# Where the chunk score products stand in a tick of a fused attention kernel

## The chip, the cores and the metric

The kernel runs on one core of one Trainium2 chip. The metric is the device time of that core in microseconds (us). A core has five engines that each work through a queue of their own, in order: TensorE (PE) for matrix products and transposes, VectorE (DVE), ScalarE (ACT), GpSimd (POOL), and SyncE (SP), from which this kernel issues its DMAs. PE's results go to PSUM; VectorE and ScalarE read PSUM and write SBUF. PEld is the weight load of a product, which can lie beside another product.

## The reference

Three stages on 8 batches of 576 tokens, with 8 heads of 64 (a width of 512). The first is attention within chunks of 64 tokens, without a mask. The second has four experts, each a causal attention over the 576 tokens of its batch with one head of 64; a token takes its two best experts, weighted by a softmax of their gate logits. The third is a layer norm and a network of 512 to 2048 to 512 with a ReLU and a residual.

```python
scores = scale * np.matmul(q_c, k_c.transpose(0, 1, 2, 4, 3))   # chunks of 64
attn = exp(scores - max); attn = attn / (sum(attn) + 1e-09)
x = np.matmul(attn, v_c)                                         # to [B, S, 512]
...
q, k, v = x @ wq[e], x @ wk[e], x @ wv[e]                        # e = 0..3
scores = np.where(causal, -1e9, scale * q @ k.T); a = softmax(scores)
out += mask[..., None] * w[:, :, kk:kk + 1] * (a @ v @ wo[e])    # the two best e
...
xn = (x - mu) / np.sqrt(var + 1e-06) * g_ln
ch = np.maximum(xn @ w_ch1, 0.0) @ w_ch2
return x + ch
```

## The kernel before

The 4608 tokens are 36 tiles of 128. A prologue (a list of steps written out by hand, to about 57 us) works on the first seven tiles; then `tick(s)` runs for s = 7 to 36, one token tile in and one out each time; the network follows, from about 490 us on. What the change touches is `tick`, in the stage from 57 to 445 us.

The pieces of work are Python generators, and `step(g)` lets a generator write its instructions up to its next `yield`. The order in which `tick` calls `step` is thus the order in which the program is written. A scheduler then orders the instructions of each engine, by and large as written but with moves of its own, and puts the waits between engines in. Each engine takes its instructions strictly in the built order.

The generators, with the tiles and lines that the prediction names:

- **Chunk attention of tile g** (`chunk_tile`, L142 to L187) has four steps. The first only takes the loaded tiles. The second writes the score products s_ps (L151, 32 products of 64x64) and the softmax over the chunk: the maximum nmc (L154) and the subtraction pc (L156) on VectorE, the exponential on ScalarE (L157), the sum and its reciprocal lc on VectorE (L159 to L161), and a multiplication on GpSimd (L162). The third transposes pc to pT_ps (L166), copied by ScalarE (pTc, L168). The fourth writes the output products x_ps (L176, 32 products of 64x64), which are taken from PSUM as a high part xTh (ScalarE, L185) and the rest xTl (VectorE, L186). Every product of the later stage is done as three of such parts.
- **Projections of a group of three tiles** (`proj_group`, L193 to L264): steps of 12 products each. A k or q step (pp, L209) ends in an eviction by ScalarE and VectorE (L212, L213 for q, L222, L223 for k), a v step (pv, L233) in L235, L236. After the last v step comes the gate.
- **Expert attention of half a token tile** (`attn_half`, L268 to L358): the two halves are the two pairs of experts. Its steps are the scores sp (L299), mask and maximum in one operation of VectorE (L312, twice), exponentials on ScalarE (L313, twice), VectorE's small l pieces (L314 to L316) and GpSimd's multiplication (L318); transposes tp (L327) with copies on ScalarE and VectorE (L329, L331); products oa_ps (L342), taken as zh and zl (L345, L346); and, in the second of a tile's halves, y_ps (L353, six products: zl with woh, zh with wol, zh with woh, for each of two pairs).
- **Weight conversion** (`narrow`, L365 to L407) goes beside it: the network's weights arrive as 64-bit numbers and are made into 32-bit ones in pieces by VectorE (L373 to L379, L384, L389), GpSimd (L381, L402) and ScalarE (L393). `bg(s)` writes one piece of it. The pieces on VectorE have to stay in the written order among one another.

PSUM has four single buffers for s_ps, pT_ps, pp, pv, tp, oa_ps and y_ps, and two double ones that sp and x_ps share. A product that needs a buffer waits until the last reader of its former content is done.

One tick has two halves. In each half come, in this order: transposes of an earlier expert half, scores of a new one, the y_ps step of a third, the chunk step of tile s, a projection step, the chunk step of tile s - 1, and the oa_ps step, with `bg(s)` between them. In the first half the chunk steps are the taking of the loaded tiles (tile s) and the transposes pT_ps (tile s - 1). In the second half they are s_ps with its softmax (tile s) and x_ps (tile s - 1). The lines are L438 to L454.

Of the kernel before, what the change touches and what calls it, by code (L numbers as in the profile page):

```python
# [22 lines left out]
def tile_kernel(ctx, tc, dims, qkt, vt, wqt, wkt, wvt, wo, g_ln, w_ch1, w_ch2, out):  # L23
# [77 lines left out]
    def load_tile(g):  # L101
        qk = se.tile([128, 2, HP, 128], F32, name="qk", bufs=3)
        vb = se.tile([128, H, D], F32, name="vb", bufs=4)
        nc.sync.dma_start(qk.rearrange("p i a t -> p (i a t)"), qkt[g])
        nc.sync.dma_start(vb.rearrange("p h d -> p (h d)"), vt[g])
        loaded[g] = (qk, vb)
# [305 lines left out]
    def step(gen):  # L412
        if gen is not None:
            next(gen, None)
# [3 lines left out]
    def bg(s, n=1):  # L418
        for _ in range(n):
            if s < CS:  # L420
                return
            if not cgen:
                if not conv:
                    return
                cgen.append(conv.pop(0)())
            if next(cgen[0], 0) == 0:
                cgen.pop()

    def tick(s, fill=None):
        if s + 2 < NT:  # L430
            load_tile(s + 2)
        if s < NT:
            chunks[s] = chunk_tile(s)
        if s >= GT + 1 and (s - GT - 1) % GT == 0 and (s - GT - 1) // GT < NT // GT:
            projs.append(proj_group((s - GT - 1) // GT))
        if s == MID - 1:
            bg(s, 999)
        for half in range(2):  # L438
            h = 2 * (s - LA) + half
            bg(s)  # L440
            step(attn.get(h - LG))
            if 0 <= h < 2 * NT:
                attn[h] = attn_half(h // 2, h % 2)
                step(attn[h])
            bg(s)
            step(attn.pop(h - LG - 1, None))
            step(chunks.get(s))
            bg(s)
            if projs:
                step(projs[0])  # L450
            bg(s)
            step(chunks.get(s - 1))
            bg(s)
            step(attn.get(h - LG))  # L454
            if projs and (s - GT - 1) % GT == 2 and half == 1:
                step(projs[0])
                projs.pop(0)
            if fill is not None:
                fill(s, half)
        chunks.pop(s - 1, None)  # L460
# [8 lines left out]
    chunks = {}  # L469
# [24 lines left out]
    for s in range(LA, MID):  # L494
        tick(s)
# [110 lines left out]
    def fill(s, half):  # L606
        next(beg, None)

    for s in range(MID, TAIL):
        tick(s, fill)  # L610
# [6 lines left out]
    for s in range(TAIL, NT + LA):  # L617
        tick(s, fill)
# [332 lines left out]
```

## Time and profile before

| | |
|---|---|
| time, median of 3 runs | 1266.5 us (1265.26 to 1267.33) |
| time of the profiled execution | 1263.14 us |
| its span in the profile | 1261.4 us |
| PE busy | 1230.1 us, 98% |
| VectorE busy | 907.1 us, 72% |
| ScalarE busy | 594.7 us, 47% |
| GpSimd busy | 265.4 us, 21% |
| granted clock of PE, mean | 0.993 |

The trace is of one execution. All times in it count from the start of the span. A row of a timeline has the start and the duration of an instruction or of a row of like instructions, its engine and line, the operation, what it writes and reads, and in brackets how long the engine stood idle before it and for whom. Products of PE overlap, so the duration of one can reach into the next; start to start is what one costs in a row. A row of waits says which engine, tile and line waited for which, for how long in total, how often, and how long at most. The granted clock is a share of the full 2.4 GHz; 0.50 is 1.2 GHz.

### The profile page before, as it was taken

How to read it: one execution, taken by the hardware profiler on the slowest of the kernel's cores; microseconds unless marked ns; L12 is line 12 of the kernel's file. 1: busy time of each engine (PE TensorE's matmuls, PEld its weight loads, DVE VectorE, ACT ScalarE, POOL GpSimd, SP SyncE). 2: the span in 40 equal slices, each digit the busy share in tenths (PEclk: the TensorE clock that was granted, in tenths of full speed). 3: DMA queues.
4: the chain of work that ended last, by engine and by line, in shares of the span. 5: the costliest groups of instructions: out<-in, count | busy, mean ns of one | idle time of the engine just before them, and what ended most of it. 6: DMA issues, size and time to landing. Idle time of an engine off the chain costs nothing.

```text
span 1261.4 us, 29453 instructions
## 1 busy us (share of the span) xinstructions
PE 1230.1 (98%) x11874; PEld 1149.3 (91%) x11874; DVE 907.1 (72%) x1957; ACT 594.7 (47%) x1171; POOL 265.4 (21%) x480
## 2 busy tenths in 40 slices
PE   7989999999999999999999999999899999999998
PEld 5878888888788887899999999999799999999998
DVE  5578777787866676996567656755797778767783
ACT  3465655566566567643343334335443433324331
POOL 2245444444542223311121202110000000000000
PEclk8999999999999999999999999999999999999999
DMA  7333434434332013655555565558865455554521
GB/s 258 104 130 116 139 116 139 139 107 148 125 106 69 28 50 126 239 196 178 179 176 170 166 196 172 166 156 257 312 200 174 138 165 159 163 175 140 168 93 42
DMA packets 95848, 191.71 MB, mean 152 GB/s; under 512 B 8544, under 2 KB 42336, under 8 KB 94816
## 3 DMA queue, kind: packets, MB, share of 16 engines
q1 hardware_dynamic: 95712, 189.83, 46.3%
q8 instruction: 93, 1.52, 0.5%
q14 instruction: 43, 0.35, 0.1%
HBM read 118.50 MB, written 71.30 MB: 150 GB/s over the span
## 4 chain that ended last, share of the span: by engine, by line
PE 84%; DVE 7%; ACT 3%; DMA 3%; POOL 1%; issue 1%; SPq 0%; DVEq 0%; POOLq 0%; ACTq 0%
PE bb L850 16%; PE bb L660 15%; PE ad L850 12%; PE ad L660 11%; PE pp L209 7%; PE pv L233 4%; PE oa_ps L342 4%; PE tp L327 4%; PE y_ps L353 4%; PE sp L299 3%; PE s_ps L151 2%; DMA w2u<-w2d 1%; PE x_ps L176 1%; PE pT_ps L166 1%; PE tp L554 1%
## 5 line engine op out<-in xcount | busy, mean ns | idle before, releaser
L660 PE MATMUL bb<-x,w1u 128*128 128x256 f32 x1728 | 217.1, 281 | 2.1 <-ACT v L681 1.6
L660 PEld LDWEIGHTS bb<-x,w1u 128*128 128x128 f32 x1728 | 209.6, 188 | 2.9 <-ACT v L681 1.9
L660 PE MATMUL ad<-x,w1u 128*128 128x256 f32 x1296 | 169.6, 282 | 1.9 <-DVE u L684 1.2
L660 PEld LDWEIGHTS ad<-x,w1u 128*128 128x128 f32 x1296 | 159.5, 188 | 2.6 <-DVE u L684 1.4
L850 PE MATMUL bb<-w2u,hn 128*128 128x256 f32 x928 | 160.3, 281 | 0.8 <-DVE xr L860 0.8
L850 PEld LDWEIGHTS bb<-w2u,hn 128*128 128x128 f32 x928 | 134.2, 189 | 1.2 <-DVE xr L860 1.0
L318 POOL TENSOR_SCALAR P<-P,l 128x128 f32<-128x128 f32 (+8 forms) x144 | 93.7, 662 | 163.2 <-DVE l L316 90.5
L850 PE MATMUL bb<-w2u,hx 128*128 128x256 f32 x640 | 125.6, 283 | 0.5 <-DVE hx L815 0.5
L313 ACT ACTIVATE P<-P,nm 128x128 f32<-128x128 f32 (+8 forms) x144 | 87.7, 611 | 72.0 <-DVE nm L312 71.6
L850 PE MATMUL ad<-w2u,hn 128*128 128x256 f32 x632 | 104.4, 281 | 0.0
L850 PEld LDWEIGHTS bb<-w2u,hx 128*128 128x128 f32 x640 | 101.0, 191 | 0.7 <-DVE hx L815 0.7
L381 POOL TENSOR_TENSOR cvt<-cva,cvt 128x512 f32<-128x512 f32 x32 | 44.3, 1385 | 238.5 <-DVE cvt L379 192.2
L850 PEld LDWEIGHTS ad<-w2u,hn 128*128 128x128 f32 x632 | 89.3, 189 | 0.0
L850 PE MATMUL ad<-w2u,hx 128*128 128x256 f32 x504 | 88.9, 280 | 0.0
L402 POOL TENSOR_TENSOR cw<-cw 128x128 f32<-128x128 f32 x128 | 61.3, 494 | 70.3 <-issue 53.6
L850 PEld LDWEIGHTS ad<-w2u,hx 128*128 128x128 f32 x504 | 74.1, 189 | 0.0
L327 PE MATMUL tp<-ident,P 128*128 128x128 f32 x464 | 66.6, 280 | 2.8 <-POOL P L318 2.7
L312 DVE CUSTOM_DVE_ANT_0 P<-sp,mcaus 128x128 f32<-128x128 f32 (+7 forms) x128 | 62.3, 516 | 7.5 <-PE sp L299 7.2
L342 PE MATMUL oa_ps<-pTa,vg 128*64 128x128 f32 x928 | 67.0, 280 | 0.3 <-ACT pTa L329 0.3
L572 DVE TENSOR_TENSOR x<-xt,x 128x512 fp32r<-128x512 f32 x63 | 49.2, 792 | 20.8 <-ACT x L571 20.8
L327 PEld LDWEIGHTS tp<-ident,P 128*128 128x128 f32 x464 | 50.0, 141 | 14.2 <-issue 8.4
L342 PEld LDWEIGHTS oa_ps<-pTa,vg 128*64 128x64 f32 x928 | 49.4, 136 | 10.7 <-issue 6.0
(236 smaller groups left out, 2643.8 us busy)
## 6 DMA issues: line engine op xcount, KB each, us to landing
qk<-in_qk SPq DMA_DIRECT2D x36, 512.0 KB, 4.1
hn<-hd SPq DMA_DIRECT2D x34, 512.0 KB, 4.4
raw<-in_w_ch SPq DMA_DIRECT2D x32, 512.0 KB, 3.9
hx<-hd SPq DMA_DIRECT2D x29, 512.0 KB, 4.4
vb<-in_v SPq DMA_DIRECT2D x36, 256.0 KB, 3.2
xs<-y SPq DMA_DIRECT2D x36, 256.0 KB, 2.0
xc<-xs SPq DMA_DIRECT2D x18, 512.0 KB, 4.6
hd<-p SPq DMA_DIRECT2D x36, 256.0 KB, 4.0
```

What stands on the lines that cost most here:

```text
L209: nc.tensor.matmul(pp, a[:, f, ws], b_[:, f, :], start=(f == 0 and n == 0), stop=(f == KF - 1 and n == 2))
L233: nc.tensor.matmul(pv, a[:, f, cs], b_[:, f, :], start=(f == 0 and n == 0), stop=(f == KF - 1 and n == 2))
L312: nc.vector.tensor_tensor_reduce(dst, src, mk, -1.0, -3.0 * NEG, OP.add, OP.min, nm[:, e2:e2 + 1])
L313: nc.scalar.activation(pe, pe, AF.Exp, bias=nm[:, e2:e2 + 1], scale=-1.0, accum_out=l[:, e2:e2 + 1])
L318: nc.gpsimd.tensor_scalar(P[e2][:, pad:W], P[e2][:, pad:W], l[:, e2:e2 + 1], 1.0, OP.mult, OP.mult)
L327: nc.tensor.transpose(tp[:, i, :], P[e2][:, kt * 128:(kt + 1) * 128], ident)
L342: nc.tensor.matmul(o_ps[e2 * HD:(e2 + 1) * HD, :], vg[:, gk % GT, e * HD:(e + 1) * HD], pT[:, e2 * n + kt, :], start=(kt == 0), stop=(kt = ...
L353: nc.tensor.matmul(y_ps, a[:, e2, :], b_[:, e2, :], start=(e2 == 0 and i == 0), stop=(e2 == EP - 1 and i == 2))
L402: nc.gpsimd.tensor_tensor(w[:, o, :], w[:, x, :], w[:, y, :], op)
L572: nc.vector.tensor_tensor(t[:, 1], tsum[i], f32(t[:, 0]), OP.subtract)
L660: nc.tensor.matmul(out[:, p], w[:, kt, a, WI[i], :], x[:, b_, kt, :], start=(start and p == 0 and kt == 0 and q == 0), stop=False, skip_gr ...
L850: ins = nc.tensor.matmul(to[:, t], x[:, c, ts], w2u[i][:, w, half * 4 + c, :], start=start, stop=False, skip_group_check=True)
```

## The change

```diff
@@ -444,11 +444,11 @@
                 step(attn[h])
             bg(s)
             step(attn.pop(h - LG - 1, None))
-            step(chunks.get(s))
             bg(s)
             if projs:
                 step(projs[0])
             bg(s)
+            step(chunks.get(s))
             step(chunks.get(s - 1))
             bg(s)
             step(attn.get(h - LG))
```

The chunk step of tile s is written behind the projection step, directly ahead of the chunk step of tile s - 1, in both halves. In the first half this moves no instruction of an engine, since that step only takes loaded tiles. In the second half it moves s_ps and the chunk softmax. It applies in the 29 ticks from s = 7 to s = 35. Three places of the built order follow.

PE, the second half of the tick that starts its s_ps at 191 us (s = 17), before:

```order
L299 MATMUL sp<-kWh,qh 128x256 x2
L151 MATMUL s_ps<-qk 64x64 x16
L209 MATMUL pp<-xTl,wqh 128x384
L209 MATMUL pp<-xTh,wql 128x384
L209 MATMUL pp<-xTh,wqh 128x384
...
L176 MATMUL x_ps<-pTc,vb 64x64 x16
L342 MATMUL oa_ps<-pTa,vg 64x128 x2
L327 MATMUL tp<-ident,P 128x128 x4
```

and now:

```order
L299 MATMUL sp<-kWh,qh 128x256 x2
L209 MATMUL pp<-xTl,wqh 128x384
L209 MATMUL pp<-xTh,wql 128x384
L209 MATMUL pp<-xTh,wqh 128x384
...
L151 MATMUL s_ps<-qk 64x64 x16
L176 MATMUL x_ps<-pTc,vb 64x64 x16
L342 MATMUL oa_ps<-pTa,vg 64x128 x2
L327 MATMUL tp<-ident,P 128x128 x4
```

The 12 products of the q step stand ahead of s_ps now, and x_ps stands directly behind it; a row without a number of times stands for one instruction, and the nine q products that are left out repeat the three. Some 20 rows further on, the six products of y_ps stood in one piece ahead of the 12 products of a v step; now eight of these stand between the third and the fourth of y_ps.

VectorE, the second half of the tick at 232 us (s = 20), where conversion pieces (cva, cvt) stand between those of the softmax, before:

```order
L154 TENSOR_REDUCE nmc<-s_ps 128x8
L156 TENSOR_TENSOR pc<-s_ps,nmc 128x512
L314 TENSOR_SCALAR l<-l 128x2
L315 RECIPROCAL l<-l 128x2
L316 TENSOR_TENSOR l<-l,wg 128x2
L373 TENSOR_SCALAR cva<-raw_3553 128x512
L159 TENSOR_REDUCE lc<-pc 128x8
L213 TENSOR_TENSOR ql<-pp,qh 128x384
...
L375 SCALAR_TENSOR_TENSOR cva<-raw_3553,cva 128x512
L186 TENSOR_TENSOR xTl<-x_ps,xTh 128x4x128
L377 TENSOR_SCALAR cvt<-cva 128x512
L346 TENSOR_TENSOR zl<-oa_ps,zh 128x128
```

and now:

```order
L314 TENSOR_SCALAR l<-l 128x2
L315 RECIPROCAL l<-l 128x2
L316 TENSOR_TENSOR l<-l,wg 128x2
L373 TENSOR_SCALAR cva<-raw_3553 128x512
L213 TENSOR_TENSOR ql<-pp,qh 128x384
L375 SCALAR_TENSOR_TENSOR cva<-raw_3553,cva 128x512
L154 TENSOR_REDUCE nmc<-s_ps 128x8
L377 TENSOR_SCALAR cvt<-cva 128x512
L156 TENSOR_TENSOR pc<-s_ps,nmc 128x512
L186 TENSOR_TENSOR xTl<-x_ps,xTh 128x4x128
L379 SCALAR_TENSOR_TENSOR cvt<-raw_3553,cvt 128x512
...
L346 TENSOR_TENSOR zl<-oa_ps,zh 128x128
```

L154 and L156 stood ahead of the three l pieces and stand behind them now, two conversion pieces further on. Between xTl and zl stand L379 and L159 (the row left out) where L377 stood; the two rows left out before are the small lc pieces L160 and L161.

VectorE, the second half of the first tick (s = 7, s_ps at 57 us), before:

```order
L154 TENSOR_REDUCE nmc<-s_ps 128x8
L314 TENSOR_SCALAR l<-l 128x2
L156 TENSOR_TENSOR pc<-s_ps,nmc 128x512
L315 RECIPROCAL l<-l 128x2
L316 TENSOR_TENSOR l<-l,wg 128x2
L213 TENSOR_TENSOR ql<-pp,qh 128x384
L159 TENSOR_REDUCE lc<-pc 128x8
```

and now:

```order
L314 TENSOR_SCALAR l<-l 128x2
L315 RECIPROCAL l<-l 128x2
L316 TENSOR_TENSOR l<-l,wg 128x2
L384 TENSOR_SCALAR cva<-raw_852 128x512
L213 TENSOR_TENSOR ql<-pp,qh 128x384
L389 SCALAR_TENSOR_TENSOR cva<-cva,cvt 128x512
L154 TENSOR_REDUCE nmc<-s_ps 128x8
L312 ISA P,nm<-sp,mcaus 128x256
L312 ISA nm 128x1
L156 TENSOR_TENSOR pc<-s_ps,nmc 128x512
```

L154 stood first in the row and stands behind two conversion pieces and the q eviction now, and L156 behind the first L312 of the half that follows.

No instruction is added or removed. On the queue of SyncE the loads of qk and vb change places with one load of conversion input in seven ticks.

## Rows read from the trace of the kernel before

**Rows 1.** The page, busy time of each engine, share of the span, instructions.

```profile
PE 1230.1 (98%) x11874; PEld 1149.3 (91%) x11874; DVE 907.1 (72%) x1957; ACT 594.7 (47%) x1171; POOL 265.4 (21%) x480
```

**Rows 2.** Waits of PE, 57 to 445 us: total us, times, longest.

```profile
PE sp L299 <- DVE xTl L186: 2.9, 3, 1.0
PE pT_ps L166 <- POOL pc L162: 2.7, 1, 2.7
PE y_ps L353 <- DVE zl L346: 0.7, 3, 0.2
```

**Rows 3.** Chain of waits, 190 to 245 us: start, duration, engine, tile, line.

```profile
192.18 0.69 DVE nmc L154
...
195.88 0.56 DVE cva L375
...
197.87 0.98 PE y_ps L353 x3
...
214.92 1.07 DVE cva L375
```

**Rows 4.** VectorE's groups by line, 57 to 445 us: busy, mean ns, idle before.

```profile
L156 DVE TENSOR_TENSOR pc<-s_ps,nmc 128x512 f32<-128x512 f32 x29 | 20.0, 690 | 0.5
```

**Rows 5.** Table by stretch, L389 alone: length, VectorE busy (times), granted clock, DMA.

```profile
57.00:371.00 314.00, 15.46 (x16) 0.99 0.39 127
```

**Rows 6.** PE's timeline, ticks at 191 and 203 us: start, duration, line, operation.

```profile
190.98 1.15 PE L151 MATMUL s_ps<-qk 64*64 64x64 f32 x32
192.06 0.44 PE L209 MATMUL pp<-xTl,wqh 128*128 128x384 f32 x1
...
194.37 0.69 PE L176 MATMUL x_ps<-pTc,vb 64*64 64x64 f32 x32
195.00 0.44 PE L342 MATMUL oa_ps<-pTa,vg 128*64 128x128 f32 x4
...
200.14 0.60 PE L166 MATMUL pT_ps<-ident,pc 128*128 128x128 f32 x4
```

**Rows 7.** PE's timeline in the prologue.

```profile
23.52 1.08 PE L151 MATMUL s_ps<-qk 64*64 64x64 f32 x29
...
25.07 1.49 PE L97 MATMUL wp<-wz 128*128 128x256 bf16 x12
```

**Rows 8.** Waits of VectorE, 66 to 375 us.

```profile
DVE l L314 <- ACT P L313: 22.0, 22, 1.4
```

**Rows 9.** ScalarE's timeline, ticks at 216 and 232 us.

```profile
219.93 0.19 ACT L313 ACTIVATION_READ_ACCUMULATOR P<-P,nm 128x1 f32 x1
...
234.71 0.19 ACT L313 ACTIVATION_READ_ACCUMULATOR P<-P,nm 128x1 f32 x1
```

**Rows 10.** VectorE's timeline, ticks at 57, 216 and 232 us.

```profile
61.40 0.68 DVE L154 TENSOR_REDUCE nmc<-s_ps 128x8 f32<-128x512 f32 x1
...
223.00 0.69 DVE L186 TENSOR_TENSOR xTl<-x_ps,xTh 128x512 fp32r<-128x512 f32 x1
...
239.37 0.28 DVE L346 TENSOR_TENSOR zl<-oa_ps,zh 128x128 fp32r<-128x128 f32 x1
```

**Rows 11.** PE's timeline, ticks at 57, 69 and 232 us; in brackets a wait.

```profile
66.78 0.66 PE L166 MATMUL pT_ps<-ident,pc 128*128 128x128 f32 x4 [2.66 <-POOL pc L162]
...
73.86 0.69 PE L176 MATMUL x_ps<-pTc,vb 64*64 64x64 f32 x32
...
239.71 0.50 PE L353 MATMUL y_ps<-woh,zl 128*128 128x512 f32 x1
```

**Rows 12.** GpSimd's timeline, tick at 191 us.

```profile
196.03 1.31 POOL L162 TENSOR_TENSOR pc<-pc,lc 128x512 f32<-128x512 f32 x1 [1.03 <-ACT zh L345]
```

**Rows 13.** Table by stretch: PE, PEld, VectorE, ScalarE, GpSimd busy; granted clock; DMA.

```profile
67.00:70.00 3.00, 2.63 (x34) 1.92 (x33) 2.15 (x11) 2.69 (x9) 2.10 (x5) 0.85 0.43 161
70.00:74.00 4.00, 4.00 (x36) 3.64 (x38) 2.67 (x7) 1.09 (x4) 1.50 (x4) 0.68 0.61 206
200.00:250.00 50.00, 48.92 (x607) 41.38 (x605) 38.56 (x118) 30.58 (x79) 24.39 (x42) 1.00 0.42 137
```

## The prediction

> **What bounds the kernel now.** I read the page first: the products of TensorE (PE) are busy for 98% of the span and VectorE (DVE) for 72% [rows 1], so what counts is any time that PE loses or saves. The change touches only the attention stage, about 57 to 445 us. There the list of PE's waits is short, 6.3 us in its three largest lines [rows 2], and these name the places where another engine is only just in time: sp (the scores of the big attention) waits for VectorE's xTl, which frees the PSUM buffer that x_ps filled; pT_ps (the transposes of the chunk softmax) waits for GpSimd's last step; y_ps waits for VectorE's zl. Two of these three are VectorE. The chain of waits of one stretch says the same [rows 3]: it leaves PE after s_ps, goes down VectorE's queue from the chunk softmax (nmc) past the weight conversion (cva), and comes back to PE at y_ps. So the second half of a tick is bound by PE, with VectorE's in-order queue close behind it.
>
> 29 ticks move a chunk (the x29 of L156, [rows 4]). In 20 of them the projection step next to it is a q product (L209), in 9 a v product (L233); I call them q ticks and v ticks. In the first tick and 15 later q ticks the weight conversion is running beside it; it makes 16 passes that are all over by 371 us (the x16 of L389, [rows 5]), so the last 4 q ticks have a quieter VectorE.
>
> **What PE gains.** In the tick at 191 us s_ps takes 1.08 us until the next products start, the q step 2.31 us until x_ps starts [rows 6]. The order of three pieces changes, not their number. What is new is that x_ps, whose tiles are also 64x64, starts directly behind s_ps. The prologue holds one such place: s_ps and x_ps together take 1.55 us from 23.52 to 25.07 [rows 7]. Apart they take 1.08 plus 0.63 us (x_ps lasts from 194.37 to 195.00, [rows 6]), 1.71 in all. A gain of 0.16 by that row; I take 0.13, since its clock was not steady. It may be 0, if a steady stretch overlaps less. 29 x 0.13 = **3.8 us gained**.
>
> **What VectorE loses.** Before, when VectorE has done the two big softmax pieces of the half (L312), it would have to wait for ScalarE's exponentials before L314. The chunk pieces L154 and L156 fill that wait. In the built order they stand behind L314 to L316, the conversion's next pieces and the q eviction (L213). VectorE then idles for the exponentials: 22 such waits exist before, in other halves, 22.0 us in all and 1.4 at most [rows 8], so 1.0 us each. The 1.38 us of L154 plus L156 (0.69 each, [rows 3, 4]) come later, in front of xTl and zl. Worked down the queue with start-to-start times of the trace:
>
> Kind A, the tick at 232 us (3 ticks). ScalarE ends the exponentials at 234.90 (234.71 plus 0.19, [rows 9]). L314 to L316 and L373 then hold VectorE until 235.75, L213 until 236.2, L375 (0.56, [rows 3]) until 236.75, L154, L377 and L156 (0.6 each) until 238.55, L186, L379 and L159 (0.6 each) until 240.35, and L346 delivers zl at 240.63. In the trace zl starts at 239.37 and is done at 239.65 [rows 10]; the second half of y_ps takes it at 239.71 [rows 11] with no slack. So 1.0 us later, or 1.4 if L375 takes 1.07 us as it did at 214.92, beside a GpSimd step, and not 0.56 as at 195.88 [rows 3]. Against a PE that would be 0.13 ahead I take 1.3 us; low 0.5, high 1.6.
>
> Kind B, the tick at 191 us (3 ticks). The same walk puts zl at 198.8 instead of 197.8, but here the built order has eight v products between the halves of y_ps, which hide it. GpSimd's step on pc is not hidden: VectorE delivers its divisor (L161) at 199.7, the step takes up to 1.31 us [rows 12], and pT_ps, at 200.14 before [rows 6], waits until about 201.0. I take 0.8 us; low 0.3, high 1.1.
>
> Kind C (5 ticks, two shapes). The next half's sp needs both PSUM buffers, so it waits for xTl. In the tick at 216 us xTl starts at 223.00 and is done at 223.69 [rows 10]; sp behind it has one of the three waits of [rows 2], 1.0 us. By the new order L384, L213, L389 (0.97, that is 15.46 over 16, [rows 5]), L154 and L156 all stand ahead of it behind exponentials that end at 220.12 [rows 9]: xTl would start at 223.55. 0.55 us later, plus 0.15 since the products of the second buffer no longer run in pairs. 0.7 us; low 0.3, high 1.0.
>
> The 4 other q ticks with conversion: in two zl comes some 0.45 us too late (0 to 0.8), in two it comes in time. In the 9 v ticks and the 4 quiet q ticks I find xTl, zl and pc in time, cost 0: there the chunk pieces meet no conversion, and VectorE's other waits are shorter.
>
> The first tick. pT_ps already waits 2.66 us here [rows 11]. L154 started at 61.40 [rows 10]; in the built order it stands behind L384, which waits for GpSimd's L381, L213 and L389. It starts near 64.75, and pc is ready near 69.9, where pT_ps started at 66.78 [rows 11]: pT_ps waits 3.1 us longer. But products that stood behind it now stand ahead: from pT_ps to x_ps, at 73.86, PE needed 7.08 us [rows 11] and needs 4.6 (1.33 for pT_ps, oa_ps and tp, of which pT_ps has 0.60 in [rows 6], 2.31 and 0.95 for the q step and s_ps). That leaves 0.6 us. After the wait before, the granted clock was 0.85 for 3 us and 0.68 for 4 us [rows 13], so the 1.2 GHz level cost 3 x 0.15 + 4 x 0.32 = 1.7 us, which are in the 7.08. The 4.6 are at full clock and the wait is longer, so I add 1.7. 2.3 net, 2.4 before the gain of 0.13; low 0.5, high 4.
>
> Sum: 3 x 1.3 + 3 x 0.8 + 5 x 0.7 + 2 x 0.45 + 2.4 = 13.1, less 3.8: **+9.3 us**. No new DMA, no new work; seven qk and vb loads swap with a load of conversion input on the queue of SyncE, both needed two ticks later, cost 0. Behind 445 us PE runs without this neighbour, so the loss is neither recovered nor grown. On the profiled execution, 1263.1 us (span 1261.4), that is 1272.4; the three runs have a median of 1266.5, and I predict on that: 1275.8.
>
> **The rivals.** *The queue has room* (0.10): VectorE is idle for 11 us of 50 from 200 to 250 us (its 38.56, [rows 13]), and if it reaches xTl and zl as early as before, only the gain stays: 1266.5 - 3.8 = 1262.7, faster. It decides at zl: in kind A a zl done by 239.6 costs nothing. Against it speak the built order and the chain of waits, which has VectorE on it already [rows 3].
>
> *Only the known waits grow* (0.14): kind C and the first tick pay, the y_ps and pT_ps waits of A and B stay within what PE loses anyway. 5 x 0.7 + 2.4 - 3.8 = +2.1: 1268.6.
>
> *The lag is handed on* (0.16): where two q ticks follow each other (216 then 232 us), VectorE enters the second one late, having no wait left in which to catch up. That brings the highs: 3 x 1.6 + 3 x 1.1 + 5 x 1.0 + 2 x 0.8 + 4 - 3.8 = +14.9: 1281.4.
>
> *The clock falls at every new wait* (0.04): if each of the 11 new waits of kinds A to C cost the 1.7 us of the first tick, +9.3 + 18.7 = +28: 1294.5. The rows speak against it: the stretch from 200 to 250 us holds the wait of 0.98 us and was granted 1.00 [rows 13]. [...]
>
> That the change doesn't do what it says is out: the built order shows it.
>
> **How the numbers follow.** The forecast has 0.56. A measurement of this kernel can tell about 0.2%, 2.5 us, from no change, so "same" is 1264.0 to 1269.0. Faster 0.10 is the first rival; same 0.17 is the second and the forecast's lowest end; slower is the rest, 0.73. The lows sum to 1.5 + 0.9 + 1.5 + 0 + 0.5 - 3.8 = +0.6, so 1267; the highs to 1281.4, and 1284 if x_ps gains a little less. 1267 to 1284 leaves out the first and the last rival and a little of the second.
>
> **What would show it.** s_ps to x_ps under 1.08 us in every changed tick (about 0.95) is the gain. In VectorE's rows a wait of over a microsecond before L314 in both halves of a tick, not in one, is the cause. New waits of PE: y_ps for zl near 1 us in 3 ticks, pT_ps for pc in 4, sp for xTl in 5 and not 3, each near 1.5 us, and a low clock for some microseconds after 70 us. If the list of PE's waits is as short as before, the first rival holds; if v ticks show waits too, the third.

## The result and the profile after

| | before | after |
|---|---|---|
| time, median of 4 runs | 1265.88 us (1263.7 to 1267.33) | 1276.1 us (1275.28 to 1278.58) |
| profiled execution, span | 1261.4 us | 1274.0 us |
| from the last x_ps of the prologue to the last x_ps (tick s = 36) | 393.94 us | 404.32 us |

The change makes the kernel slower: ratio 1.0088, 95% interval 1.0076 to 1.0100, some 10.2 us. The prediction was 1275.8 us, in a range of 1267 to 1284.

The third line of the table is the stage of the change, cut at two products that both kernels have. It is used for all kernels below, since it leaves out what differs from one execution to the next behind the stage. Each such figure is of one profiled execution, and a fall of the granted clock in the first tick, of another length in some of the profiles, is in it. The stage grew by 10.4 us. The two profiled spans differ by 12.6; the other 2 us lie behind the stage, in waits of the network, which the change does not touch.

The page of the kernel after, its line of busy times (us, share of the span, instructions), answers to [rows 1]:

```profile
PE 1230.0 (97%) x11874; PEld 1146.3 (90%) x11874; DVE 906.5 (71%) x1957; ACT 590.7 (46%) x1171; POOL 267.7 (21%) x480
```

PE is as busy as before, to 0.1 us, in a span that is longer: the time went into waits. Its waits from 57 to 460 us (total us, times, longest) answer to [rows 2], and VectorE's before L314, from 57 to 380 us, to [rows 8]:

```profile
PE pT_ps L166 <- POOL pc L162: 7.8, 4, 5.0
PE sp L299 <- DVE xTl L186: 3.6, 3, 1.2
PE tp L327 <- DVE pc L156: 2.0, 3, 0.7
PE pp L209 <- DVE kWl L223: 1.1, 3, 0.4
PE y_ps L353 <- DVE zl L346: 0.8, 4, 0.2
```

```profile
DVE l L314 <- ACT P L313: 44.7, 46, 1.5
```

Three of the five lines of PE are of before: pT_ps grew from 2.7 to 7.8 us, sp from 2.9 to 3.6, y_ps hardly (0.7 to 0.8). tp and pp are new. The list holds waits of 0.15 us and more; shorter ones, and products that run one behind the other where they ran side by side, cost some of the rest. VectorE waits for the exponentials in 46 halves where it waited in 22 (of a stretch that is 14 us shorter): in nearly every half, where it was one in two.

Now the tick that the prediction called kind A, the one at 232 us before (s = 20). VectorE in the kernel after (start, duration, line, operation, in brackets idle time before it):

```profile
241.03 0.17 DVE L314 TENSOR_SCALAR l<-l 128x2 f32<-128x2 f32 x1 [1.06 <-ACT P L313]
...
242.31 0.82 DVE L375 SCALAR_TENSOR_TENSOR cva<-raw,cva 128x512 int32<-128x512 int32 x1
243.05 0.68 DVE L154 TENSOR_REDUCE nmc<-s_ps 128x8 f32<-128x512 f32 x1
...
244.00 0.67 DVE L156 TENSOR_TENSOR pc<-s_ps,nmc 128x512 f32<-128x512 f32 x1
244.59 0.68 DVE L186 TENSOR_TENSOR xTl<-x_ps,xTh 128x512 fp32r<-128x512 f32 x1
...
246.38 0.28 DVE L346 TENSOR_TENSOR zl<-oa_ps,zh 128x128 fp32r<-128x128 f32 x1
```

and PE, the same tick, from s_ps to the next pT_ps:

```profile
240.47 1.08 PE L151 MATMUL s_ps<-qk 64*64 64x64 f32 x29
241.34 0.27 PE L176 MATMUL x_ps<-pTc,vb 64*64 64x64 f32 x1
...
244.82 0.41 PE L327 MATMUL tp<-ident,P 128*128 128x128 f32 x2 [0.68 <-DVE pc L156]
...
246.72 0.50 PE L353 MATMUL y_ps<-woh,zl 128*128 128x512 f32 x1
...
249.21 0.66 PE L166 MATMUL pT_ps<-ident,pc 128*128 128x128 f32 x4
```

s_ps and x_ps are one piece, 0.87 us from the one to the other. s_ps is done near 241.6, but L154 starts at 243.05: ahead of it stand the wait for the exponentials (1.06 us, ended at 241.03), the l pieces, L373, L213 and L375. xTl and zl are as late as the walk had them: before, x_ps started at 235.45 and zl was done at 239.65 [rows 10], 4.2 us on; now zl is done at 246.66, 5.3 us behind the start of x_ps. PE loses 0.68 us at 244.82, where tp waits for a PSUM buffer that s_ps fills until L156 has read it (244.67), and the rest in small pieces at y_ps, in the v products and at pT_ps.

### The profile page after: what moved, and what is told of

It reads as the page before. It is cut to its first block, busy times and chain, and to the rows that moved or that the text cites. A ratio compares the mean times of both kernels' runs of the same rounds, so it can differ in the third digit from the quotient of the medians.

```text
span 1274.0 us, 29466 instructions
## 1 busy us (share of the span) xinstructions
PE 1230.0 (97%) x11874; PEld 1146.3 (90%) x11874; DVE 906.5 (71%) x1957; ACT 590.7 (46%) x1171; POOL 267.7 (21%) x480
## 4 chain that ended last, share of the span: by engine, by line
PE 62%; DMA 3%; DVE 3%; ACT 2%; issue 1%; POOL 1%; SPq 0%; ACTq 0%; DVEq 0%; POOLq 0%
PE bb L850 15%; PE bb L660 14%; PE ad L850 12%; PE ad L660 10%; PE pp L209 2%; PE oa_ps L342 2%; PE tp L327 2%; PE y_ps L353 1%; PE pv L233 1%; DMA hx<-hd 1%; PE sp L299 1%; PE tp L554 1%; DMA hd<-u 1%; DMA w2u<-w2d 1%; POOL P L318 1%
## 5 line engine op out<-in xcount | busy, mean ns | idle before, releaser
L318 POOL TENSOR_SCALAR P<-P,l 128x128 f32<-128x128 f32 (+8 forms) x144 | 98.7, 697 | 142.0 <-DVE l L316 50.4
L312 DVE CUSTOM_DVE_ANT_0 P<-sp,mcaus 128x128 f32<-128x128 f32 (+7 forms) x128 | 62.3, 511 | 7.8 <-PE sp L299 4.6
```

The source lines that it names most:

```text
L312: nc.vector.tensor_tensor_reduce(dst, src, mk, -1.0, -3.0 * NEG, OP.add, OP.min, nm[:, e2:e2 + 1])
L318: nc.gpsimd.tensor_scalar(P[e2][:, pad:W], P[e2][:, pad:W], l[:, e2:e2 + 1], 1.0, OP.mult, OP.mult)
```

## Experiments

Four questions: is it VectorE's queue or the lateness of the products (1), is it the wait for the exponentials (2), is it the conversion (3, 4), and does every tick pay (5 to 7). The last part tries the pair in the other place.

**1. Products as before, softmax late.** The softmax steps of VectorE go behind the projection step, the l pieces and the conversion, as in the kernel after; s_ps stays where it was. In 19 of 28 ticks xTl now stands between L154 and L156, and pc comes 0.1 to 1.4 us later behind x_ps than in the kernel after. (Line numbers shift by up to 4.)

```diff
+        yield                       # behind the s_ps products
-        nc.vector.tensor_reduce(nm, s3, AX.X, OP.max, negate=True)
+        keep(g)(nc.vector.tensor_reduce(nm, s3, AX.X, OP.max, negate=True))
...
             if projs:
                 step(projs[0])
             bg(s)
+            if half == 1:
+                step(chunks.get(s))
             step(chunks.get(s - 1))
```

> The products s_ps stay ahead of the projection step, where they were before the change. Only VectorE's two chunk softmax pieces (L154, L156) are written behind the projection step and held behind the three l pieces (L314 to L316) and the conversion pieces, as the changed kernel has them. If VectorE's queue is the cause, the loss stays and the gain of x_ps directly behind s_ps (0.15 us a tick, 29 ticks, 4.5 us) is missing: 1276 plus 4.5, about 1280 us, 1273 to 1284. If the lateness of the products themselves is the cause, the softmax finds its products ready and the time stays near that of the kernel before, 1264 to 1268 us.

Measured: 1283.72 us, ratio 1.0161 (1.0137 to 1.0184); the stage takes 413.22 us, 19.3 more than before. Its PE waits from 57 to 460 us:

```profile
PE pT_ps L170 <- POOL pc L166: 12.3, 14, 5.3
```

With products that are early and a softmax that is late, the loss is there, and larger. The place in VectorE's queue makes it, not the lateness of s_ps. (s_ps also holds its PSUM buffer for longer here; what that costs was not separated.) pc is late in many more ticks, and pT_ps pays 14 times. Of the 8.9 us that the stage takes more than in the kernel after, 4.5 are the missing gain of the pair, and some 1.8 a longer low clock in the first tick (0.81 granted from 62 to 80 us, 0.91 after).

**2. The l pieces later.** The kernel after, with a `yield` ahead of L314 in the expert half, and that step taken behind the projection.

```diff
             nc.scalar.activation(pe, pe, AF.Exp, ..., accum_out=l[:, e2:e2 + 1])
+        yield
         nc.vector.tensor_scalar(l, l, 1e-9, None, OP.add)
...
             step(chunks.get(s))
+            step(attn.get(h))
             step(chunks.get(s - 1))
```

> The changed kernel, but the three l pieces and GpSimd's multiplication of each expert half are written behind the projection step instead of directly behind the exponentials, so that VectorE has conversion pieces to do while the exponentials run. The products keep the changed order. If VectorE's wait for the exponentials is the cause, its 46 waits before L314 (44.7 us) shrink by half or more and about 0.9 of the 1.3 us of a late tick come back: 1266 to 1270 us. If the lateness of the products is the cause, nothing comes back: 1275 to 1278 us.

Measured: 1274.96 us, ratio 1.0079 (1.0064 to 1.0094); the stage takes 404.55 us. Hardly anything came back. The waits and the clock say why. VectorE from 57 to 380 us; PE's timeline at the tick of kind C (s = 10); the stretch behind it (length, busy PE, PEld, VectorE, ScalarE, GpSimd, then granted clock, DMA share, GB/s):

```profile
DVE l L315 <- ACT P L313: 24.3, 26, 2.8
```

```profile
106.51 0.41 PE L299 MATMUL sp<-kWh,ql 64*128 64x320 f32 x1 [1.48 <-DVE xTl L186]
```

```profile
108.00:112.00 4.00, 4.00 (x14) 3.57 (x13) 1.90 (x8) 2.33 (x5) 1.04 (x1) 0.57 0.35 135
```

VectorE's waits for the exponentials did shrink, from 44.7 to 24.3 us. But in this tick they still take 0.64 us, and the conversion piece ahead of L154 (L390) takes 1.04 us where L389 takes 0.71 after: xTl is no earlier, and sp waits 1.48 us (1.20 after). Behind that wait the clock was granted 0.57 for four microseconds, mostly its 1.2 GHz level, and the same happened in the two other ticks of this shape. From x_ps to x_ps this tick takes 17.59 us, 15.95 in the kernel after: three such ticks lose 5.0 us more than there. Without that the stage would be 4.7 shorter than after, and without the longer low clock of its first tick (0.81 granted from 62 to 80 us, 0.91 after, some 1.8 us) 6.5. By this estimate the filled wait is worth more than half of the 10.4 us, which the clock took back, so the wait for the exponentials is part of the cause. The expectation that filling it brings the time down fell.

**3. Conversion in the first halves only**, two pieces at a place, with the old and with the new order.

```diff
     def bg(s, n=1):
+        if n == 1:
+            n = 2 - 2 * half_now[0]         # 2 in the first half, 0 in the second
```

> The kernel before, but all pieces of the weight conversion are written in the first halves of the ticks, two at a place, none in the second halves. It is the reference for the next kernel. VectorE has the same work; the first halves hold more of it: 1264 to 1272 us.

> The changed kernel with all conversion pieces in the first halves, two at a place. In the second halves L154 stands directly behind L213 and no conversion piece ahead of xTl and zl. If the conversion pieces are what makes xTl, zl and pc late, the moved chunk step costs nothing there any more and only its gain stays: 1 to 4 us faster than the kernel with the conversion moved alike and the old order. If the waits for the exponentials are enough by themselves, it is 4 us or more slower than that kernel.

Measured: 1273.73 us (ratio 1.0069, 1.0048 to 1.0091) and 1283.85 us (ratio 1.015, 1.0134 to 1.0165). The second is 10.1 slower than the first, which speaks against the conversion. It does not settle it: the first halves are overloaded now, VectorE enters the second halves late, and PE waits for it in other places. PE's waits of the second kernel, 57 to 460 us, and one of its stretches:

```profile
PE tp L327 <- DVE ql L213: 5.7, 5, 1.5
```

```profile
234.00:240.00 6.00, 5.16 (x24) 4.30 (x25) 4.39 (x14) 3.45 (x7) 1.24 (x2) 0.72 0.41 132
```

tp waits for a buffer that the q eviction holds (and 2.8 us for the k eviction), a wait that the list of the kernel after doesn't have. Beside the first tick, the clock falls in three places of the stage here (0.72 in the stretch shown, 0.79 from 184 to 192 us, 0.62 from 360 to 369), and in one of the first kernel (0.72 from 346 to 358 us), worth 3.4 us of the 10.1. This pair is inconclusive.

**4. No conversion in the stage, and conversion behind the softmax.** First the old and the new order with the whole conversion in one row at the end of the attention (`CS = 36`).

> The kernel before, with no weight conversion beside the attention: all of it is done in one row at its end (the last tick). The end of the stage becomes longer in this kernel and in the next alike, so they are read against one another. VectorE loses the conversion pieces from 57 to 440 us, so PE's waits there shrink below the 6 us of before.

> The changed kernel, with the conversion in one row at the end as in the kernel just named. If the conversion pieces in front of the chunk softmax are what makes the loss, only the gain of 0.15 us a tick is left: 2 to 5 us faster than that kernel, and quiet ticks all along. If the products' lateness, the exponentials and the buffers in PSUM are enough, it is slower than that kernel by 3 us or more, with waits of PE for pc, xTl and zl as now.

Measured: 1349.58 and 1355.01 us; the row at the end costs some 85 us in both (PE waits 83.6 us in it in the one, 89.2 in the other), so the totals say nothing on the stage. The stage does. PE's timeline, first and last x_ps of the old order, then of the new:

```profile
49.81 0.69 PE L176 MATMUL x_ps<-pTc,vb 64*64 64x64 f32 x32
...
432.70 0.69 PE L176 MATMUL x_ps<-pTc,vb 64*64 64x64 f32 x32
```

```profile
50.54 0.69 PE L176 MATMUL x_ps<-pTc,vb 64*64 64x64 f32 x32
...
434.09 0.69 PE L176 MATMUL x_ps<-pTc,vb 64*64 64x64 f32 x32
```

382.89 and 383.55 us: the new order costs 0.7 us where it cost 10.4. The first tick loses 1.6 us and the next two 0.6; the others win 1.6 together. The 1.6 us are the clock: behind a wait of pT_ps of 1.91 us in the first tick it fell with the new order, behind 1.53 us it did not with the old one. From 62 to 80 us, old order first:

```profile
62.00:80.00 18.00, 16.46 (x195) 13.45 (x194) 11.93 (x44) 11.55 (x33) 5.33 (x9) 1.00 0.20 62
```

```profile
62.00:80.00 18.00, 16.03 (x156) 12.90 (x156) 11.48 (x40) 10.18 (x28) 5.61 (x10) 0.91 0.24 86
```

Without that fall the new order would win some 0.9 us. The 2 to 5 us of the expectation are not there: in three v ticks tp waits for the copy of pT_ps (1.1 us in all), and no conversion is there to cause it.

Then, the kernel after with the conversion left in place, but in the second halves written behind the oa_ps step:

```diff
             step(attn.pop(h - LG - 1, None))
-            bg(s)
+            if half == 0:
+                bg(s)
             if projs:
                 step(projs[0])
-            bg(s)
+            if half == 0:
+                bg(s)
             step(chunks.get(s))
             step(chunks.get(s - 1))
             bg(s)
             step(attn.get(h - LG))
+            if half == 1:
+                bg(s)
+                bg(s)
```

> The changed kernel, and in the second halves the two conversion pieces that stood ahead of the chunk softmax are written behind the oa_ps step. VectorE then goes from L316 and L213 straight to L154, L156 and xTl. If it is the place of the conversion pieces in VectorE's queue, most of the 11 us come back and the gain shows: 1262 to 1268 us. If not, 1273 or more.

Measured: 1267.52 us, ratio 1.0017 (1.0007 to 1.0027); the stage takes 396.40 us. 8 of the 10.4 us are back. PE's and VectorE's waits:

```profile
PE pT_ps L166 <- POOL pc L162: 3.6, 1, 3.6
...
PE sp L299 <- DVE xTl L186: 1.6, 3, 0.6
```

```profile
DVE l L314 <- ACT P L313: 43.2, 47, 1.3
```

VectorE waits for the exponentials as in the kernel after (43.2 us), yet PE hardly waits for pc and xTl: pT_ps once, in the first tick, and sp half as long as before the change. So the wait alone costs little. It costs where conversion pieces stand between it and the chunk softmax.

**5. Only the ticks that the prediction had at cost 0**: the 9 v ticks and the 4 without conversion.

```diff
+            late = (s - GT - 1) % GT == 2 or not (conv or cgen)
+            if not late:
+                step(chunks.get(s))
...
+            if late:
+                step(chunks.get(s))
             step(chunks.get(s - 1))
```

> The changed order only in the 9 ticks with a v step and the 4 with no conversion left; the other 16 as before. If those ticks hold the gain alone and the loss comes only from the ticks with conversion, the time is 1.5 to 2 us below the kernel before (13 times 0.15 us). If the moved step costs in every tick, it is 2 us or more above.

Measured: 1268.68 us, ratio 1.0028 (1.0018 to 1.0038): slower by 3.7, where 1.5 to 2 faster was expected. PE's timeline in the tick behind the v tick s = 9, which itself has the old order:

```profile
95.24 0.44 PE L327 MATMUL tp<-ident,P 128*128 128x128 f32 x2 [0.55 <-ACT pTc L168]
...
96.95 1.15 PE L151 MATMUL s_ps<-qk 64*64 64x64 f32 x32 [0.38 <-DVE kWl L223]
```

In the kernel before, tp does not wait here, and s_ps waits 0.09 us. tp waits for the copy of pT_ps, s_ps for kWl: both are waits for a PSUM buffer. Which buffer a tile gets is fixed when the kernel is built, and moving s_ps in one tick changed who follows whom in the next. 1.1 us are lost there from x_ps to x_ps, behind s = 9, 18 and 27 alike, and 0.3 behind s = 12 and 21. Another 0.7 us went in the first tick, which is as before, to a longer low clock (below).

**6. The same without s = 9, 18 and 27.**

```diff
-            late = (s - GT - 1) % GT == 2 or not (conv or cgen)
+            late = s % PT and ((s - GT - 1) % GT == 2 or not (conv or cgen))
```

> As the kernel with the changed order in 13 ticks, less s = 9, 18 and 27, whose s_ps the half after next follows with waits of tp for pTc and of s_ps for kWl. If the 1.05 us behind each of these three ticks are what made that kernel slower, about 2.6 us come back: 1265 to 1267 us, no more than 1.5 above the kernel before. If the loss of that kernel lies elsewhere, it stays 3 to 4 us above.

Measured: 1266.15 us, ratio 1.0003 (0.9992 to 1.0013). Some 2.5 us are back, so those three ticks made most of the loss of experiment 5. Against the kernel before the change no difference can be told.

**7. The first tick as before**, the other 28 as in the kernel after.

```diff
+            if s == LA:
+                step(chunks.get(s))
...
+            if s > LA:
+                step(chunks.get(s))
             step(chunks.get(s - 1))
```

> The changed kernel with the first tick (s = 7) left as before. If the longer wait of pT_ps for pc there (5.0 us instead of 2.7) costs what the comparison of the traces gives, 1 to 1.5 us come back: 1274 to 1275 us. By the prediction's term for it, 2.3 us come back: 1273 to 1274.

Measured: 1277.66 us, ratio 1.0099 (1.0083 to 1.0114): not better than the kernel after. PE's timeline of that kernel at the tick of kind C (s = 10), and its stretches there; then the same place of the kernel after:

```profile
105.68 0.42 PE L299 MATMUL sp<-kWh,ql 64*128 64x320 f32 x2 [1.20 <-DVE xTl L186]
```

```profile
104.00:108.00 4.00, 2.80 (x16) 2.11 (x16) 3.90 (x10) 2.35 (x6) 2.10 (x5) 0.88 0.88 340
108.00:112.00 4.00, 4.00 (x17) 3.69 (x16) 1.30 (x6) 2.33 (x5) 1.32 (x2) 0.69 0.38 147
```

```profile
106.09 0.42 PE L299 MATMUL sp<-kWh,ql 64*128 64x320 f32 x2 [1.20 <-DVE xTl L186]
```

```profile
104.00:108.00 4.00, 2.80 (x19) 2.05 (x18) 3.90 (x9) 2.56 (x6) 2.50 (x5) 1.00 0.82 276
108.00:112.00 4.00, 4.00 (x32) 3.67 (x32) 2.21 (x9) 3.25 (x7) 1.55 (x2) 1.00 0.60 233
```

The same wait of 1.20 us, once followed by a clock of 0.88 and 0.69 and once by 1.00. Two of the three ticks of this shape lost some 1.6 us that way in this execution and none in the kernel after. From the x_ps of the prologue to that of s = 9 this kernel is 1.3 us ahead of the kernel after, although its first tick itself paid more to the clock (below). Then the falls at the ticks of kind C take it back. The four runs were granted 0.988 to 0.991 on the mean, those of the kernel after 0.989 to 0.995. The expectation looked at one tick and had not reckoned with the clock at the others.

**8. The pair ahead of the projection step.** The old place of s_ps, and x_ps brought up to it; once in all ticks, once from s = 9 on. The step of tile s - 1 moves in both halves, so in the first half pT_ps comes ahead of the projection step too.

```diff
             step(chunks.get(s))
+            step(chunks.get(s - 1))
             bg(s)
             if projs:
                 step(projs[0])
             bg(s)
-            step(chunks.get(s - 1))
```

> The other way to put the two products side by side: s_ps stays ahead of the projection step and x_ps comes up to it, so that x_ps follows s_ps directly and both stand ahead of the projection. The gain of the pair should be there (0.15 us a tick, 4.5 us), xTl comes earlier, and L154 and L156 still fill the wait for the exponentials: 1260 to 1264 us by the theory of VectorE's queue. Against it: x_ps needs a double buffer that sp holds until VectorE's L312 is done, so where sp took both, PE waits for L312 without the projection step as cover, up to 1 us in some 10 ticks: then 1266 to 1272 us.

> As the kernel with x_ps brought up to s_ps, but from s = 9 on; the ticks s = 7 and 8 keep the old order. The 1.05 us that the second of these had lost by the time of its y_ps come back: 1258 to 1260 us, about 6 to 7 below the kernel before. If the first ticks are not what lost it, it stays 5 to 6 us below.

Measured: 1259.77 us, ratio 0.9954 (0.9939 to 0.9969), and 1258.62 us, ratio 0.9953 (0.9940 to 0.9965). Both are faster than the kernel before, by some 6 us, the first a little more than expected. They cannot be told apart, so what the first ticks are worth here stays open. PE's and VectorE's waits of the first, 57 to 460 and 57 to 380 us:

```profile
PE pT_ps L166 <- POOL pc L162: 4.6, 1, 4.6
...
PE x_ps L176 <- DVE nm L312: 0.3, 1, 0.3
```

```profile
DVE l L314 <- ACT P L313: 21.0, 23, 1.4
```

L154, L156 and xTl fill the wait for the exponentials again (21.0 us of waits, as before the change). The cost that I feared, x_ps waiting for a buffer of sp, is small: in 7 of the 28 ticks x_ps starts 1.02 to 1.45 us behind s_ps and not 0.87, and only one of these shows as a wait (0.3 us). In these 7 the gain of the pair is all or mostly missing.

So the pair alone does not make the 6.4 us by which the stage is shorter than before (387.51). Half of them lie in the ticks s = 10, 19 and 28: xTl comes earlier with x_ps, and the wait of sp for it, one of the known waits of before (2.9 us in all), is gone. From s_ps to s_ps each of these ticks is 1.1 us shorter. PE's timeline at s = 10, before and here:

```profile
103.19 0.41 PE L299 MATMUL sp<-kWh,ql 64*128 64x320 f32 x1 [0.97 <-DVE xTl L186]
```

```profile
102.56 0.41 PE L299 MATMUL sp<-kWh,ql 64*128 64x320 f32 x2
```

What the earlier pT_ps is worth was not tested.

## Why the prediction was right, and where not

**The gain of the pair** was there and a little larger. In a tick without conversion (s = 31 to 32) x_ps follows x_ps after 12.77 us before and 12.61 after. PE's timelines, the two starts of each:

```profile
382.60 0.69 PE L176 MATMUL x_ps<-pTc,vb 64*64 64x64 f32 x32
...
395.37 0.69 PE L176 MATMUL x_ps<-pTc,vb 64*64 64x64 f32 x32
```

```profile
392.81 0.27 PE L176 MATMUL x_ps<-pTc,vb 64*64 64x64 f32 x2
...
405.42 0.27 PE L176 MATMUL x_ps<-pTc,vb 64*64 64x64 f32 x1
```

0.16 us a tick, forecast 0.13; in all 28 pairs x_ps starts 0.87 us behind s_ps. The row of the prologue had given 0.16, and nothing was to be taken off for the clock: 1.00 was granted there from 23.0 to 25.1 us. The gain was counted 29 times, but the first tick has no x_ps (that of tile 6 is done in the prologue): 28 x 0.16 = 4.5, forecast 3.8.

**What VectorE loses**, by kind, from x_ps to x_ps in the two traces, with 0.16 added back for the gain (but for s = 35, which ends at an x_ps without s_ps):

| kind | ticks | forecast, us | measured, us | sum forecast | sum measured |
|---|---|---|---|---|---|
| A (s = 11, 20, 29) | 3 | 1.3 | 1.2, 1.4, 1.2 | 3.9 | 3.9 |
| B (s = 8, 17, 26) | 3 | 0.8 | 1.1, 1.1, 1.1 | 2.4 | 3.3 |
| C (s = 10, 19, 28; 14, 23) | 5 | 0.7 | 0.5 to 0.6 | 3.5 | 2.7 |
| other q ticks with conversion | 4 | 0.45, 0 | 0.4 in two, 0 in two | 0.9 | 0.8 |
| v ticks | 9 | 0 | 0.6 in three, 0.25 in two | 0 | 2.3 |
| q ticks without conversion | 4 | 0 | 0.4 in the last | 0 | 0.4 |
| first tick | 1 | 2.4 | 1.5 | 2.4 | 1.5 |

13.1 forecast, 14.9 measured, less 3.8 and 4.5: +9.3 and +10.4. Kinds A to C, which carry the sum, were sized about right. What the sum lacked (the v ticks and the last q tick 2.7, kind B 0.9) was made up for the larger part by what it had too much (the first tick 0.9, kind C 0.8, and 0.7 in the gain). That part of the agreement is luck, and so is the rest of it, down to 0.3 us: the prediction stands on a median of three runs that is 0.6 us above that of four.

**Kind A, B, C.** The walk down VectorE's queue held to within 0.1 us in kind A. The place did not: forecast was y_ps waiting for zl, seen is first tp, waiting for the PSUM buffer of s_ps. L156 is late by the same queue, and it stands ahead of zl; I had followed what reads a result and not what waits for a buffer. In kind B pT_ps waits 0.92 us, as forecast; the GpSimd step took its share and the term was at its high end.

In kind C xTl starts 0.58 us later behind x_ps (s = 19: 3.69 us, 3.11 before), forecast 0.55, and the ticks lose 0.52 to 0.56, without the 0.15 on top. The two shapes pay in two ways. In s = 10, 19 and 28 sp waits 1.20 us, only 0.23 more than before, since a product of sp that ran ahead of that wait now stands behind it. In s = 14 and 23 there is no wait of PE to see: until xTl is done, the products of the one sp buffer run without those of the other beside them. The twelve take 1.80 us where they took 1.27, by PE's timeline at s = 14, the first of sp and the y_ps behind the last, before and after:

```profile
156.90 0.39 PE L299 MATMUL sp<-kWh,ql 64*128 64x288 f32 x1
...
158.17 0.50 PE L353 MATMUL y_ps<-woh,zl 128*128 128x512 f32 x1
```

```profile
160.40 0.40 PE L299 MATMUL sp<-kWh,ql 64*128 64x288 f32 x1
...
162.20 0.50 PE L353 MATMUL y_ps<-woh,zl 128*128 128x512 f32 x1
```

**The cause** holds in the form that the prediction gave it: the pieces of the chunk softmax stand behind the exponentials and the conversion. Shown: with early products and a late softmax the loss stays (experiment 1); without conversion it is 0.7 us, with a fall of the clock of 1.6 in it (experiment 4); with the conversion behind the softmax 8 of 10.4 us come back though VectorE waits for the exponentials as long. Of the two halves of the argument, the wait for the exponentials and the conversion pieces behind it, neither makes the whole loss alone: with the conversion gone or behind the softmax all but 0.7 and 2.5 us go while the wait stays, and with the wait filled some 6.5 us of it go, the clock left aside, while the conversion stays (experiment 2). The prediction's sign for its cause, a wait before L314 in both halves of a tick, is there in the kernel of experiment 4 as well, which loses next to nothing. It was too weak a sign.

**The v ticks and the quiet ticks** are the step that failed: "I find xTl, zl and pc in time, cost 0". In the v ticks they are. But behind the v ticks s = 9, 18 and 27 the q product of the next tick comes directly behind sp, without the 1.08 us of s_ps as a cover, and waits 0.39 us for a buffer that kWl (L223) holds (before, s_ps waited 0.09 for it). Another 0.3 go in tp, whose fifth product waits for the copy of pT_ps. With the old order in s = 10, 19 and 28 and the new one in the v ticks it is worse, 1.1 us (experiments 5 and 6). It is the assignment of PSUM buffers that the order of the program changes, a term that the sum did not have. That the assignment is behind it is read from the tiles that the waits name; no run changed the assignment alone. In the two v ticks of 0.25 us the loss is in tp again: its ninth product starts 0.30 us behind the eighth, right behind the end of kWl, where 0.11 is usual. In the last q tick zl is not in time, against the forecast: it is done 3.3 us behind x_ps, 2.3 before, and the six products of y_ps take 1.83 us and not 1.49. By the table these ticks are worth about 2.7 us together.

**The first tick.** The wait of pT_ps grew from 2.66 to 5.0 us, 2.4 and not 3.1 more; counted from the x_ps of the prologue pT_ps is 2.6 us later. From there to x_ps PE took 5.76 us, where the terms of the prediction come to 6.3 (4.6 and 1.7 for the low clock). The wait and the products were both sized too high. PE's timeline, and two stretches that answer to [rows 13]:

```profile
69.01 1.12 PE L166 MATMUL pT_ps<-ident,pc 128*128 128x128 f32 x4 [5.02 <-POOL pc L162]
```

```profile
67.00:70.00 3.00, 0.99 (x4) 0.72 (x4) 1.13 (x8) 0.41 (x2) 1.95 (x3) 0.82 0.39 153
70.00:74.00 4.00, 4.00 (x21) 3.36 (x22) 1.92 (x10) 2.36 (x7) 0.29 (x1) 0.71 0.00 0
```

0.82 and 0.71, where 0.85 and 0.68 were granted before: 3 x 0.18 + 4 x 0.29 = 1.7 us, as the prediction had it. The clock falls once, for the same time, after a wait of 2.66 or of 5.02 us.

**The rivals.** The queue had no room. Kinds A and B cost 7.2 us, so it was not only the known waits that grew. The lag is not handed on: the tick behind each tick of kind C costs what the walk gave it alone. The clock did not fall at the new waits of kinds A to C, with 1.00 granted from 80 to 455 us; but experiments 2, 3 and 7 show that it can after a wait of 1.2 to 1.6 us, so the rival was nearer than its chance of 0.04 said. The Trainium skill's page "TensorE: Matmul & The Clock Gate" (section "HAM oscillation") tells of a kernel that is throttled anew at every wait between two bursts of products; its waits, for a DMA, are longer than those of kinds A to C here. The kernel of experiment 2 was throttled behind three waits of only 1.48 us, the kernel after, behind waits of up to 1.20, not once outside the first tick.

## What to carry to other kernels

Products of one engine that are cheaper side by side can be brought together in two ways. Here the one that moved x_ps up, with xTl earlier for it, gained 6 us, and the one that moved s_ps down lost 10: look at what each makes early or late on the other engines. A piece that fills a wait of another engine's in-order queue has a worth that no row of busy times shows: before it is moved, look what stands behind it in that queue and what fills the wait then. When an order changes, follow the buffers too, tile by tile: who held this one before, and what covered that wait. A loss need not show as a wait: products that ran side by side and no longer do cost as much (kind C).

## What the runs showed of the hardware

- A wait of PE of 1.2 to 1.6 us, in a stretch that is otherwise full, can be followed by a fall of the granted clock to its 1.2 GHz level that costs about 1.6 us. At the same place, sp in the ticks s = 10, 19 and 28, it came in 3 of 3 ticks behind 1.48 us, in 2 of 3 behind 1.20 in one kernel (experiment 7) and in 0 of 3 behind 1.20 in another (the kernel after), and in only 1 of 3 behind 1.6 us in the first kernel of experiment 3, there for twice as long. What decides between them was not found.
- The length of a wait alone does not set how long the clock stays low. In the first tick the low clock cost nothing (after a wait of pT_ps of 1.5 us), about 1.6 us (18 us at 0.91) or 3.4 us (18 us at 0.81), and nothing between: 1.6 after waits of 1.9, 2.7, 3.6, 4.6 and 5.0 us, 3.4 after 2.7, 3.9, 4.1, 4.3 and 5.3. Two kernels with the same wait of 2.7 us, the one before and that of experiment 5, from 62 to 80 us:

```profile
62.00:80.00 18.00, 14.73 (x138) 11.91 (x136) 14.09 (x44) 9.90 (x29) 8.60 (x14) 0.91 0.30 104
```

```profile
62.00:80.00 18.00, 15.08 (x134) 11.77 (x133) 13.55 (x43) 9.66 (x26) 8.08 (x14) 0.81 0.31 102
```

The columns are as in the stretches above; the granted clock is 0.91 and 0.81.
